# Sequences 1 to 3 of an SSD and MLP kernel: B by token through SBUF transfers, x by chunk, copies on other engines

## The chip, the cores and the metric

The kernel runs on one core of a Trainium2 chip. The metric is the time of one execution on the device in microseconds. Before the change it was 119.97 us, the median of 3 runs (119.9 to 120.58). The profile shows one execution that took 118.98 us, of which 117.0 us lie between its first and its last instruction (the span). The engines are named as in the profile: PE (matrix multiplication; PEld are its weight loads), DVE (vector engine), ACT (scalar engine), POOL, and SP, which here only issues transfers.

## What is computed

Two things in a row: a chunked state-space layer over 4 sequences with 8 heads, and a two-layer MLP on its result.

```
batch, H, S, D, N = 4, 8, 768, 32, 16
for each chunk:
    cum  = cumsum(log a)
    M    = (C B^T) * exp(cum_i - cum_j) * causal
    y    = M x + (C state) * exp(cum)
    state = exp(sum log a) * state + sum_j B_j x_j exp(cum_last - cum_j)
x2 = y as (3072 tokens, 256)
out = gelu_tanh(x2 @ w_in) @ w_out          # 256 -> 2048 -> 256
```

## The kernel before

The kernel takes chunks of 128 tokens, so that a sequence has 6 (`CPB`) and the whole input 24. Chunks are worked in units: unit 0 is chunk 0, unit 1 is chunk 1, and units 2 to 12 are two chunks each. Sequence b starts at chunk 6b; sequence 1 is units 4 to 6, and so on.

All work is first written down as nodes: a function, an engine, an assumed duration, the nodes it depends on. `run_order` then plays the nodes through in assumed time, with a priority for each node from the table `PRIO`, and the instructions are emitted in the order that comes out. Each engine runs its own list in that order. SP is one list too: loads and stores wait there one behind the other. Each transfer also waits until the transfer eight before it on the same list has landed, because eight completion counters are used in turn.

For a unit u the steps are:

- `f_G` (L659, PE): the products of C and B for each pair of heads, into the PSUM tile gb (four banks, one per head group).
- `f_M` (L669, DVE): gb times the causal mask, to the SBUF tile m.
- `f_D` (L680, PE): the chunk's contribution to the state, from B by token (the tile bn) and x, into a buffer of the ring hp.
- `f_S` and `f_SP` (L730, L737, DVE): the new state, and the state spread out over a block mask.
- `f_Y` (L702 and L711, PE): y from the state and from m and x, into the PSUM tile yb. From unit 4 on, Y of u, D of u + 1 and G of u + 1 are one block, `f_YDG`.
- `f_yev` (L720): yb copied to xm, the input of the MLP.
- `f_s1` (L757, PE): w_in times xm, into hp; `f_gelu` (L765, ACT): hp through gelu into gT. There are two hp buffers.
- `f_s2` (L774, PE): gT times w_out into o_ps (one bank) or yb; `f_oev` (L781, L783): that copied to SBUF; `f_store` (L787): to memory. The last chunk is done in two halves of 128 columns: `f_s2h`, `f_oevh`, `f_storeh` (L792 to L801).

For each sequence, B and C are scaled by the running products of a. For sequences 1 to 3 they come with tokens spread over partitions in a way that a 32 by 32 transpose on DVE can turn: `f_mulg` (L533) multiplies, `f_Tg` (L543) transposes to bh and ch (token along the free axis), `f_Fg` (L553) makes ce from ch. B by token, which `f_D` needs, is then made out of bh by PE: `f_N` (L625) is six transposes into gb, `f_bn` (L458 through `copy`, ACT) copies them to bn. Sequence 0 goes another way (`f_T`, `f_E`, `f_F`, and `f_N` for chunks 1 to 5).

x of sequences 1 to 3 comes as one transfer per sequence (`load_xs`, L353), x of sequence 0 unit by unit. `f_castx` (L460, POOL) casts it to bf16. `f_wi` and `f_wo` cast the weights, which come in quarters through six buffers wf; w_in quarters 2 and 3 are shared by POOL and DVE (L462).

While PE has nothing to do before the first s2, it is given fill multiplications (L1065).

Of the kernel before, what the change touches and what calls it, by code (L numbers as in the profile page):

```python
# [31 lines left out]
def run_order(nodes, pools, hop=0.08, same=0.04, idle=None, wait=()):  # L32
# [64 lines left out]
    'f_clip(0, 256)': 308.538, 'f_R(0,)': -15.941, 'f_clip(256, 384)': -339.826, 'f_RT0()': 1159.49,  # L97
    'f_R(1,)': 367.141, 'f_recip0()': -323.896, 'f_mul0(1,)': -323.906, 'f_mul0(0,)': -35.176,
    'f_T0(1,)': 1123.21, 'f_T0(0,)': 1159.5, 'f_ce0()': -138.371, 'f_bh0()': 266.725, 'f_R(2,)': 330.337,
    'f_G(0,)': -91.981, 'f_pe()': -193.992, 'f_RT()': 1125.27, 'f_M(0, 0, 0, 2)': -285.936,  # L100
    'f_M(0, 0, 2, 4)': 367.131, 'f_pp()': 1125.26, 'f_recip()': 468.131, "f_castx(0, 'ACT')": 266.715,
    'f_mul(1,)': -194.002, 'f_pend()': 270.364, 'f_Y(0,)': 1119.78, 'f_yev(0,)': 209.42,
    'f_mul(0,)': -35.176, 'f_T(1,)': 1152.81, "f_wi(0, 0, 2, 'POOL')": 97.158,
    "f_E(0, 1, 'ACT', 21, 64)": 270.354, 'f_T(0,)': 55.447, "f_E(0, 1, 'ACT', 64, 128)": 272.36,
    'f_F(0, 128, 384)': 468.121, 'f_D(0,)': 1170.19, 'f_s1(0, 0)': 1244.43,
    "f_E(0, 0, 'ACT', 21, 64)": -152.035, 'f_F(0, 384, 768)': -343.397, "f_wi(1, 0, 2, 'POOL')": 106.043,
    "f_E(0, 0, 'ACT', 64, 128)": 102.425, 'f_S(0, 0)': -318.328, 'f_G(1,)': 1209.63, 'f_SP(0,)': -323.654,
    'f_gelu(0, 0)': 267.9, 'f_N(0,)': 1123.2, "f_castx(1, 'POOL')": 106.053, 'f_M(1, 0, 0, 4)': -287.074,
    'f_s1(0, 1)': 1244.44, "f_bn(0, 'ACT')": 270.405, 'f_D(1,)': 1119.09, 'f_gelu(0, 1)': 103.579,
    'f_G(2,)': 379.65, "f_wi(2, 0, 1, 'POOL')": -96.227, "f_wi(2, 1, 2, 'DVE')": 244.836,  # L110
    'f_S(1, 0)': 509.234, 'f_Y(1,)': 1167.76, 'f_SP(1,)': -318.348, 'f_s1(0, 2)': -68.513,
    'f_yev(1,)': -185.791, "f_wi(3, 0, 1, 'POOL')": 97.168, "f_wi(3, 1, 2, 'DVE')": -166.728,
    'f_gelu(0, 2)': 88.559, 'f_M(2, 0, 0, 4)': 468.111, 'f_s1(0, 3)': 256.892, 'f_s1(1, 0)': -5.424,
    'f_gelu(0, 3)': 841.948, 'f_M(2, 1, 0, 4)': 286.612, "f_castx(2, 'POOL')": 106.083,
    'f_gelu(1, 0)': 209.42, 'f_s1(1, 1)': 1244.44, 'f_D(2,)': -72.563, 'f_gelu(1, 1)': 310.499,
    'f_G(3,)': 1170.77, "f_wo(0, 'POOL')": -6.862, 'f_S(2, 0)': -86.636, 'f_s1(1, 2)': 1167.75,
    'f_SP(2,)': -328.534, 'f_S(2, 1)': -166.718, 'f_Y(2,)': 1125.08, 'f_gelu(1, 2)': -187.491,
    'f_SP(3,)': -95.439, "f_wo(1, 'POOL')": 106.093, 'f_s1(1, 3)': 39.343, 'f_M(3, 0, 0, 4)': 471.605,
    'f_yev(2,)': 310.489, "f_s2(0, 0, 0, 'o')": 1244.43, "f_s2(0, 0, 1, 'o')": 1149.98,
    'f_gelu(1, 3)': 43.879, "f_wo(2, 'POOL')": 71.86, 'f_s1(2, 0)': 262.608, 'f_M(3, 1, 0, 4)': -59.147,  # L120
    'f_s1(2, 1)': 1158.13, 'f_gelu(2, 0)': 316.947, "f_s2(0, 0, 2, 'o')": -169.949,
    "f_wo(3, 'POOL')": -209.595, 'f_gelu(2, 1)': 45.731, 'f_s1(2, 2)': 1170.19, 'f_s1(2, 3)': -203.565,
    'f_gelu(2, 2)': -95.091, "f_s2(0, 0, 3, 'o')": 1161.73, "f_castx(3, 'POOL')": 106.073,
    'f_gelu(2, 3)': -187.501, 'f_s1(2, 4)': -116.936, 'f_clipg(1,)': -328.524, 'f_scang(1,)': -182.29,
    "f_oev(0, 'ACT')": 316.957, 'f_s1(2, 5)': -331.499, 'f_gelu(2, 4)': 69.73, 'f_rT(1,)': 1150.59,
    "f_s2(1, 0, 0, 'o')": -206.245, 'f_qT(1,)': -105.019, "f_s2(1, 0, 1, 'o')": 281.291,
    'f_gelu(2, 5)': -281.439, 'f_D(3,)': -165.791, 'f_s1(2, 6)': 215.528, 'f_mulg(1, 0, 0, 3)': -276.921,
    "f_s2(1, 0, 2, 'o')": 348.67, 'f_S(3, 0)': -197.187, 'f_gelu(2, 6)': -234.888,
    "f_s2(1, 0, 3, 'o')": -86.131, 'f_SP(4,)': -161.739, 'f_s1(2, 7)': -124.52,
    'f_mulg(1, 0, 3, 6)': -104.486, "f_oev(1, 'ACT')": 253.329, 'f_Y(3,)': -102.426, 'f_store(0,)': 1122.82,  # L130
    'f_gelu(2, 7)': -70.863, 'f_Tg(1, 0, 0, 3)': -94.76, "f_s2(2, 0, 0, 'o')": -163.857,
    'f_Tg(1, 0, 3, 6)': -94.74, 'f_yev(3,)': -250.819, "f_s2(2, 0, 1, 'o')": -198.132,
# [12 lines left out]
    'f_gelu(3, 5)': -106.495, 'f_SP(6,)': -136.64, "f_s2(3, 0, 1, 'o')": 253.321, 'f_s1(3, 6)': 85.42,
    'f_SP(7,)': -49.121, 'f_YDG(4,)': -223.29, 'f_scang(2,)': 68.177, 'f_gelu(3, 6)': -185.039,
    'f_rT(2,)': 65.364, 'f_s1(3, 7)': 213.456, 'f_S(5, 0)': -126.73, 'f_yev(4,)': 98.262,
    "f_s2(3, 0, 2, 'o')": 1165.93, 'f_store(3,)': -294.692, 'f_S(5, 1)': -120.802, 'f_gelu(3, 7)': -337.135,
    'f_mulg(2, 0, 3, 6)': -75.966, 'f_s1(4, 0)': 228.601, 'f_s1(4, 1)': 90.433, 'f_SP(9,)': -67.877,
    'f_gelu(4, 0)': -346.344, "f_s2(3, 0, 3, 'o')": 272.801, 'f_M(5, 0, 0, 4)': -66.78,  # L150
    'f_gelu(4, 1)': 58.961, 'f_s1(4, 2)': 1244.61, "f_oev(4, 'ACT')": 264.536, 'f_s1(4, 3)': -243.335,
    'f_gelu(4, 2)': 104.018, "f_s2(3, 1, 0, 'o')": 281.251, 'f_M(5, 1, 0, 4)': -146.018,
    "f_s2(3, 1, 1, 'o')": 282.52, 'f_gelu(4, 3)': 264.546, 'f_s1(4, 4)': 228.611, 'f_SP(8,)': -52.003,
    "f_castx(8, 'POOL')": -310.299, 'f_s1(4, 5)': -138.071, 'f_gelu(4, 4)': -233.107,
    "f_s2(3, 1, 2, 'o')": 316.331, 'f_mulg(2, 0, 0, 3)': -31.787, "f_castx(7, 'POOL')": 290.955,
    "f_s2(3, 1, 3, 'o')": 266.119, 'f_gelu(4, 5)': 344.271, 'f_Tg(2, 0, 3, 6)': 24.233,
    'f_s1(4, 6)': -159.257, "f_castx(9, 'POOL')": 297.549, 'f_Tg(2, 0, 0, 3)': 61.636,
    "f_oev(5, 'ACT')": 58.931, 'f_store(4,)': -314.436, 'f_YDG(5,)': 280.254, 'f_qT(2,)': 68.167,
    'f_gelu(4, 6)': 97.521, 'f_mulg(2, 1, 3, 6)': -119.373, 'f_s1(4, 7)': 282.53, 'f_S(6, 0)': -96.547,
    'f_yev(5,)': 9.537, "f_s2(4, 0, 0, 'o')": 1165.94, 'f_M(6, 0, 0, 4)': -96.449,  # L160
    "f_s2(4, 0, 1, 'o')": 1264.77, 'f_gelu(4, 7)': -346.334, 'f_s1(5, 0)': -163.07, 'f_s1(5, 1)': 269.011,
    'f_M(6, 1, 0, 4)': -258.554, 'f_gelu(5, 0)': -66.058, "f_s2(4, 0, 2, 'o')": 282.52,
    'f_store(5,)': -360.018, "f_s2(4, 0, 3, 'o')": 281.261, 'f_gelu(5, 1)': 206.319, 'f_s1(5, 2)': 292.499,
    'f_mulg(2, 1, 0, 3)': -53.518, "f_oev(6, 'ACT')": 206.339, 'f_s1(5, 3)': -242.892,
    'f_gelu(5, 2)': 417.866, 'f_Tg(2, 1, 0, 3)': 31.703, 'f_N(2,)': 287.685, 'f_SP(10,)': 40.492,
    "f_s2(4, 1, 0, 'o')": 294.667, 'f_gelu(5, 3)': -342.46, "f_s2(4, 1, 1, 'o')": -145.414,
    'f_Fg(2, 0, 3)': 40.502, "f_bn(2, 'ACT')": 52.208, 'f_s1(5, 4)': 266.109, 'f_Tg(2, 1, 3, 6)': 114.6,
    'f_s1(5, 5)': -159.026, 'f_Fg(2, 3, 6)': 1189.33, 'f_gelu(5, 4)': 195.675, "f_s2(4, 1, 2, 'o')": 389.998,
    'f_clipg(3,)': 1208.58, "f_s2(4, 1, 3, 'o')": -178.482, 'f_gelu(5, 5)': 398.02,
# [83 lines left out]
def kernel(  # L253
# [491 lines left out]
    def f_s1(u, i):  # L745
# [4 lines left out]
        if u not in gts:  # L750
            gts[u] = next_gt()
# [351 lines left out]
```

## Time and profile before

| what | value |
|---|---|
| median of 3 runs | 119.97 us |
| the profiled execution | 118.98 us |
| its span | 117.0 us |
| mean granted PE clock | 0.995 |
| s1, L757, 128x256 forms | x352, 47.8 us busy |
| s2, L774, into o_ps | x336, 44.4 us busy |
| gelu, L765 | x96, 53.6 us busy, 596 ns each |
| M, L669, 128x1024 | x23, 27.2 us busy, 1213 ns each |
| f_N of sequences 1 to 3, L625 into gb | x18 |
| f_bn of sequences 1 to 3, L458 from gb | x3, 815 ns each |
| transfers | 14.28 MB, mean 122 GB/s |

Busy times of PE overlap (a multiplication is counted from its start to the end of its pipeline), so 267 ns of mean length is not what one costs in a row: the chain shows eight 128x256 multiplications in 0.87 us.

The page cuts the span in 40 slices; a digit is the busy share of a slice in tenths:

```
PE   5899999999999999999999999999999999999980
DVE  3787999939699996994999693291919000000100
ACT  4123756765795778687666859667777776676610
POOL 7303735640032003200510000000000000000000
DMA  2998979968959497579611101101101101111111
```

Read from left to right, these rows show an opening of some seven slices, a middle in which PE is full and DVE nearly so, and an end in which only PE and ACT work. The DMA row falls away after slice 20, when all loads have come.

### The profile page before, as it was taken

The numbers are of one execution on the slowest core, as the hardware profiler recorded it, in microseconds if no ns is written. First come the engines' busy times: TensorE is split into PE (matmuls) and PEld (weight loads), VectorE is DVE, ScalarE is ACT, GpSimd is POOL, SyncE is SP. The second block draws the span as 40 slices with busy tenths as digits, with TensorE's granted clock in tenths as the row PEclk, the third lists the DMA queues.
The fourth block names the chain that finished last, engine by engine and source line by source line (L and its number), as shares of the span: only waits on it lengthen the run. The fifth ranks groups of instructions, "written<-read, shape, count | busy, mean of one in ns | idle before, by whom it ended". The sixth has DMA issues, their size and how long they took to land.

```text
span 117.0 us, 3536 instructions
## 1 busy us (share of the span) xinstructions
PE 111.7 (96%) x1484; PEld 98.9 (85%) x1484; DVE 71.2 (61%) x161; ACT 75.3 (64%) x145; POOL 18.1 (16%) x38
## 2 busy tenths in 40 slices
PE   5899999999999999999999999999999999999980
PEld 5788778997987897998989899898989899999970
DVE  3787999939699996994999693291919000000100
ACT  4123756795765778687666859667777776676610
POOL 7303735640032003200510000000000000000000
PEclk9999999999999999999999999999999999999998
DMA  2998979968959497579611101101101101111111
GB/s 49 251 287 233 364 180 375 313 153 188 207 137 218 112 210 169 117 186 208 172 46 45 44 7 45 41 12 45 50 0 45 50 0 44 45 50 45 46 47 45
DMA packets 44251, 14.28 MB, mean 122 GB/s; under 512 B 39052, under 2 KB 42700, under 8 KB 44236
## 3 DMA queue, kind: packets, MB, share of 16 engines
q1 hardware_dynamic: 43148, 13.95, 48.4%
q10 hardware_dynamic: 1088, 0.11, 0.7%
q8 instruction: 11, 0.18, 0.6%
q14 instruction: 4, 0.03, 0.1%
HBM read 10.91 MB, written 3.15 MB: 120 GB/s over the span
## 4 chain that ended last, share of the span: by engine, by line
PE 87%; DVE 7%; POOL 2%; issue 1%; ACT 1%; POOLq 0%; DVEq 0%; ACTq 0%
PE hp L757 35%; PE o_ps L774 31%; PE gb L659 3%; PE yb L774 3%; DVE m L669 3%; PE yb L711 3%; PE yb L702 3%; PE o_ps L1065 2%; PE gb L792 2%; DVE ce L619 1%; PE hp L492 1%; PE gb L625 1%; DVE sp_new L737 1%; DVE w_in_sb L462 1%; PE hp L680 1%
## 5 line engine op out<-in xcount | busy, mean ns | idle before, releaser
L765 ACT ACTIVATE gT<-hp 128x512 bf16<-128x512 f32 x96 | 53.6, 596 | 20.0 <-PE hp L757 19.9
L757 PE MATMUL hp<-xm,w_in_sb 128*128 128x256 bf16 (+1 forms) x416 | 53.0, 267 | 0.0
L757 PEld LDWEIGHTS <-w_in_sb 128*128 128x128 bf16 x416 | 42.0, 115 | 3.3 <-issue 2.1
L774 PE MATMUL o_ps<-w_out_sb,gT 128*128 128x256 bf16 x336 | 44.4, 273 | 0.0
L774 PEld LDWEIGHTS <-gT 128*128 128x128 bf16 x368 | 35.8, 98 | 3.6
L669 DVE TENSOR_TENSOR m<-gb,tri 128x1024 bf16<-128x1024 f32 (+1 forms) x25 | 28.5, 1171 | 0.0
L783 DVE COPY o_sb<-o_ps 128x256 f32<-128x256 f32 x1 | 0.4, 425 | 18.5 <-ACT gT L765 18.5
L781 ACT ACTIVATE o_sb<-o_ps 128x256 f32<-128x256 f32 x20 | 7.7, 386 | 4.9 <-ACT gT L765 3.2
L737 DVE SCALAR_TENSOR_TENSOR sp_new<-s_new,pend,bmask 128x256 bf16<-128x256 f32 x20 | 10.3, 526 | 0.3
L1065 PE MATMUL o_ps<-wz 128*128 128x128 bf16 x75 | 8.9, 281 | 1.3 <-DVE warm L364 1.3
L460 POOL CAST x<-xs_t 128x512 bf16<-128x512 f32 x9 | 5.6, 654 | 27.6 <-DMA xs_t<-in_x_dram 18.1
L730 DVE SCALAR_TENSOR_TENSOR s_new<-s_new,pend,hp 128x64 f32<-128x64 f32 x16 | 4.5, 279 | 7.3 <-PE hp L680 4.4
L720 ACT ACTIVATE xm<-yb 128x512 bf16<-128x512 f32 (+1 forms) x13 | 7.3, 563 | 2.4 <-PE yb L711 2.2
L1065 PEld LDWEIGHTS <-wz 128*128 128x128 bf16 x75 | 6.9, 129 | 1.6 <-DVE warm L364 1.3
L711 PE MATMUL yb<-m,x 128*32 128x128 bf16 x192 | 6.3, 223 | 0.0
L702 PE MATMUL yb<-ce,sp_new 128*32 128x128 bf16 x160 | 5.3, 221 | 0.0
L659 PE MATMUL gb<-ce,bh 32*128 32x256 bf16 x96 | 5.2, 282 | 0.1
L533 DVE TENSOR_TENSOR bc<-bc_t,rr 128x192 bf16<-128x192 f32 x12 | 4.6, 435 | 1.0 <-DMA bc_t<-in_C_dram 0.9
L460 POOL CAST w_in_sb<-wf 128x512 bf16<-128x512 f32 x6 | 3.7, 636 | 8.4 <-DMA wf<-in_moe_w_in_dram 8.4
L460 POOL CAST w_out_sb<-wf 128x1024 bf16<-128x1024 f32 x4 | 4.2, 1040 | 2.4 <-DMA wf<-in_moe_w_out_dram 2.4
L711 PEld LDWEIGHTS <-x 128*32 128x32 bf16 x192 | 3.8, 97 | 0.8 <-issue 0.8
L702 PEld LDWEIGHTS <-sp_new 128*32 128x32 bf16 x160 | 2.9, 96 | 1.7 <-issue 1.6
(83 smaller groups left out, 67.3 us busy)
## 6 DMA issues: line engine op xcount, KB each, us to landing
out_dram<-o_sb SPq DMA_DIRECT2D x23, 128.0 KB, 1.8
xs_t<-in_x_dram SPq DMA_DIRECT2D x3, 768.0 KB, 6.6
wf<-in_moe_w_in_dram SPq DMA_DIRECT2D x4, 512.0 KB, 7.0
wf<-in_moe_w_out_dram SPq DMA_DIRECT2D x4, 512.0 KB, 6.4
bc_t<-in_B_dram SPq DMA_DIRECT2D x12, 96.0 KB, 2.8
bc_t<-in_C_dram SPq DMA_DIRECT2D x12, 96.0 KB, 2.3
x_t<-in_x_dram SPq DMA_DIRECT2D x6, 128.0 KB, 7.3
bc_t<-in_C_dram SPq DMA_DIRECT2D x1, 384.0 KB
```

The lines of the kernel that those rows point to most:

```text
L460: nc.gpsimd.tensor_copy(out=o, in_=i)
L659: nc.tensor.matmul(out=gb[:, g, 256 * k:256 * k + 256], lhsT=bh_of(gc)[32 * g:32 * g + 32], rhs=ce_of(gc)[32 * g:32 * g + 32], start=True, ...
L669: nc.vector.tensor_tensor(out=MT[gc][:, g0:g1], in0=gb[:, g0:g1, 256 * k:256 * k + 256] .rearrange("p g (e t) -> p g e t", e=2), in1=tri_b ...
L702: nc.tensor.matmul(out=y4[32 * j:32 * j + 32, k, w], lhsT=sp[:, 32 * h:32 * h + 32], rhs=ce_of(gc)[:, h % 2], start=first(j), stop=False, ...
L711: nc.tensor.matmul(out=y4[32 * j:32 * j + 32, k, w], lhsT=X16[u][:, k, 32 * h:32 * h + 32], rhs=m[:, h // 2, h % 2, :], start=first(j), st ...
L720: nc.scalar.activation(xm[:, :, t0:t0 + n * Q].rearrange("p w (c t) -> p c w t", c=n), y4[:, 0:n], AF.Copy)
L737: nc.vector.scalar_tensor_tensor(out=sp_new.rearrange("p (g d) -> p g d", g=4), in0=state[("s", gc)].rearrange("p (o d) -> p o d", o=1).to ...
L757: nc.tensor.matmul(out=hp[:, j * nt:(j + 1) * nt], lhsT=w_in5[:, kc, fi // 4, fi % 4], rhs=xm[:, kc, t0:t0 + nt], start=(kc == 0), stop=(k ...
L765: nc.scalar.activation(gts[u][:, i * per:(i + 1) * per, 0:nt], hps.pop((u, i)).rearrange("p (j t) -> p j t", j=per), AF.Gelu_apprx_tanh)
L774: nc.tensor.matmul(out=ops[gc], lhsT=gts[u][:, fi, tt * Q:(tt + 1) * Q], rhs=w_out_sb[:, fi, :], start=(fi == 0), stop=(fi == NF - 1), ski ...
L781: nc.scalar.activation(o_sb, ops.pop(gc), AF.Copy)
L1065: nc.tensor.matmul(out=zb[:, 0:128], lhsT=wz[:, 0:128], rhs=wz[:, 0:128], start=True, stop=True)
```

## The change

- **B by token.** For sequences 1 to 3 `f_N` and `f_bn` go. After `f_mulg` of B, `f_bq` copies the scaled B into a tile bq in two strided halves (the first half of sequence 1's and both of the others' on POOL, one on ACT), and four transfers per sequence, `load_bn`, move it from SBUF to SBUF into bn, which now lies by head group. They are issued on SP. `f_D` reads bn there.
- **x by chunk.** x of sequences 1 to 3 is loaded in six transfers of 128 KB each instead of one. x of sequence 0 lies in one tile of six chunks. The order of the loads comes from the priorities: the first chunks of x come before B of sequence 0, and two more x chunks come before the last quarter of w_in and of w_out.
- **Buffers.** wf is one tile of six slots with fixed places, which also holds x, B and C of sequence 3 later; gT is three tiles that hold two units each; bn has a buffer for each sequence.
- **Output of chunks 0 and 1.** They share the one bank of o_ps, each in its half, and their s2 are interleaved.
- **Last halves.** `f_s2h` writes into the two buffers of hp instead of gb.
- **Copies' engines.** Each copy may now run on several engines; the table `ENG` picks one. To DVE go eight output copies, three x casts, three half quarters of w_out, two of the four `f_E` copies of sequence 0, and the last `f_yev`; to ACT go the output copy of chunk 21, two x casts and halves of w_in quarters 0 and 3. All priorities are new.

```diff
-    next_bn = ring(const, 2, [128, CPB, 128], BF16, "bn")
+    next_bn = ring(const, batch, [128, CPB * 128], BF16, "bn")
+    next_bq = ring(const, 2, [128, R, CPB, 2 * N], BF16, "bq")
...
-    def load_xs(b):
-        XF[("s", b)] = ldxs.tile([128, H * CPB, D], FP32, name="xs_t")
-        nc.sync.dma_start(out=XF[("s", b)], in_=bass.AP(
-            tensor=x.tensor, offset=x.offset + b * H * S * D, ap=[[D, Q], [Q * D, H * CPB], [1, D]]))
+    def load_xs(b, c):
+        XF[("s", b)] = xst[b - 1].rearrange("p (k d) -> p k d", d=D)
+        nc.sync.dma_start(out=XF[("s", b)].rearrange("p (h c) d -> p c h d", c=CPB)[:, c],
+                          in_=x[b, :, c * Q:(c + 1) * Q, :].rearrange("h p d -> p h d"))
...
+    def f_bq(b, k, eng):
+
+
+        if k == 0:
+            U[b]["bq"] = next_bq()
+        copy(eng, U[b]["bq"].rearrange("p (s k) c n -> p k s c n", k=2)[:, k],
+             bc16_of(b, 0).rearrange("p (c s n k) -> p k s c n", s=2, n=2 * N, k=2)[:, k])
+
+    def load_bn(b, g):
+
+        d = U[b]
+        if "bn" not in d:
+            d["bn"] = next_bn()
+        nc.sync.dma_start(out=d["bn"][:, 192 * g:192 * g + 192],
+                          in_=d["bq"][32 * g:32 * g + 32].rearrange("p r c n -> p r (c n)"))
...
     def f_s2h(h):
+        ops[("h", h)] = next_hp()[:, 0:128]
         for f in range(NF):
-            nc.tensor.matmul(out=gb[:, 2 * h, 0:128], lhsT=gts[NU - 1][:, f, Q:2 * Q],
+            nc.tensor.matmul(out=ops[("h", h)], lhsT=gts[len(BLOCKS) - 1][:, f, Q:2 * Q],
                              rhs=w_out_sb[:, f, 128 * h:128 * h + 128], start=(f == 0),
-                             stop=(f == NF - 1), skip_group_check=True)
+                             stop=(f == NF - 1))
...
-        nn = add("PE", 0.34, f_N, b, deps=ts, prio=q + 15.6)
-        bb = add("ACT", 0.75, f_bn, b, "ACT", deps=[nn], prio=-45)
-        nn.takes("gram", bb)
-        for c in range(CPB):
-            bnn[CPB * b + c] = bb
+        bq = []
+        for k in range(2):
+            bq.append(any_of({"ACT": 0.6, "POOL": 0.8, "DVE": 0.5}, f_bq, b, k, deps=mb + bq, prio=q - 0.5))
+        for n in bnl[b]:
+            n.deps += bq
...
+ENG = {
+    'f_castx(1,)': 'ACT', 'f_E(0, 1, 64, 128)': 'DVE', 'f_wi(0, 1)': 'ACT', 'f_E(0, 0, 21, 64)': 'DVE',
+    'f_wi(3, 1)': 'ACT', 'f_wo(0, 1)': 'DVE', 'f_wo(2, 0)': 'DVE', 'f_wo(3, 0)': 'DVE', 'f_oev(1,)': 'DVE',
+    'f_bq(1, 0)': 'POOL', 'f_castx(5,)': 'ACT', 'f_castx(7,)': 'DVE', 'f_bq(2, 0)': 'POOL',
+    'f_oev(5,)': 'DVE', 'f_bq(2, 1)': 'POOL', 'f_castx(8,)': 'DVE', 'f_castx(9,)': 'DVE',
+    'f_bq(3, 0)': 'POOL', 'f_oev(9,)': 'DVE', 'f_bq(3, 1)': 'POOL', 'f_oev(11,)': 'DVE', 'f_oev(12,)': 'DVE',
+    'f_oev(16,)': 'DVE', 'f_oev(17,)': 'DVE', 'f_yev(12,)': 'DVE', 'f_oev(20,)': 'DVE', 'f_oev(21,)': 'ACT',
+}
```

## The prediction

> **What bounds the kernel now.** The page first: shares of engines, and shares of the chain that ended last.
>
> ```profile
> PE 111.7 (96%) x1484; PEld 98.9 (85%) x1484; DVE 71.2 (61%) x161; ACT 75.3 (64%) x145; POOL 18.1 (16%) x38
> ...
> PE 87%; DVE 7%; POOL 2%; issue 1%; ACT 1%; POOLq 0%; DVEq 0%; ACTq 0%
> ```
>
> TensorE holds the chain, but not all the time, so I read the chain in order of time (start, length, engine, tile, line):
>
> ```profile
> 11.69 1.65 DVE ce L619 x4
> ...
> 15.14 0.24 issue
> 15.38 0.29 DVE s_new L730
> 15.69 0.48 DVE sp_new L737
> 16.17 0.75 DVE w_in_sb L462
> 16.93 2.27 DVE m L669 x2
> ...
> 30.41 0.34 PE gb L625 x6
> ...
> 36.02 0.17 PE hp L680 x8
> ...
> 50.13 0.34 PE gb L625 x6
> ...
> 71.00 0.33 PE gb L625 x6
> ...
> 111.77 1.80 PE gb L792 x32
> 113.66 0.30 DVE o_sb L462
> 114.03 0.28 ACT o_sb L458
> ```
>
> Three stages are to be seen. Until about 19.2 us DVE leads (after loads) and PE's fill multiplications only pass the time. From 19.24 to 113.57 us every piece is PE's, back to back, so here a microsecond of PE work removed is one gained, and any wait of PE is lost for good. Then a tail: two copies one behind the other, and a store, to the span's end at 117.0.
>
> Third, the busy time of the engines in stretches, because the change gives DVE more work (columns: PE, PEld, DVE, ACT, POOL busy, clock, DMA):
>
> ```profile
> 25.00:30.00 5.00, 5.00 (x74) 4.08 (x73) 4.00 (x12) 3.60 (x8) 0.61 (x1) 1.00 0.92 189
> 30.00:35.00 5.00, 5.00 (x55) 4.36 (x54) 4.15 (x11) 3.34 (x7) 1.05 (x2) 1.00 0.89 169
> 35.00:45.00 10.00, 10.00 (x130) 8.72 (x127) 9.79 (x24) 6.98 (x14) 0.74 (x2) 1.00 0.93 187
> 60.00:70.00 10.00, 10.00 (x159) 8.81 (x146) 9.00 (x20) 7.35 (x14) 0.00 (x0) 1.00 0.09 28
> ```
>
> DVE has 0.2 us to spare in 35 to 45 and 1.0 in 60 to 70, and PE still never waits.
>
> **The change part by part.**
>
> *Transposes out (f_N, f_bn).* Eighteen L625 transposes leave PE: 0.34 + 0.34 + 0.33 = 1.01 us of the gapless chain. Three bn copies (0.81 us each) leave ACT, which is busy 64%, so they count nothing. All other PE counts are the same in both orders (416 of s1, 368 + 32 of s2, 192 + 160 of Y, 96 of G, 80 of D), but for 8 fills fewer before 20 us. Gain 1.01.
>
> *Last halves in two buffers.* Now both halves lie in one tile, gb. The DVE copy starts 0.09 us after the last of 32 L792 multiplications although its own half was done 0.9 us earlier, and the ACT copy starts only when DVE's has ended. With a tile for each half, DVE copies beneath the second half and ACT starts where DVE did: 114.03 - 113.66 = 0.37 us gained. The store behind it is the same.
>
> *B by token.* In place of a PE pass, two strided copies (bq) per sequence and four SBUF-to-SBUF transfers on SP's queue. No row shows a 128x384 bf16 copy on POOL; POOL's 128x512 cast at 0.65 bounds it above, ACT's 128x384 copy of 0.49 below. The tightest use is sequence 1's: its B multiplication ends on DVE at 29.2, PE needs bn at 36.02. In the new DVE order a w_out cast (which waits for its load) and an output copy stand ahead of that multiplication's second half: 0.4 + 0.4, so 30.0. POOL's bq 0.65, ACT's 0.4 behind it: 31.1. On SP the first transfer waits for bq, and with it everything queued behind: two stores between the four transfers, then two x chunks and the next sequence's a, B and C. Six issues at 0.41 to 0.50 (stores 0.41, bc loads 2.0 for 4) make 33.7. Landing: nearest rows are stores (1.8) and 96 KB loads of B (2.8), so 35.5 to 36.5 against 36.0. I take 0, the middle of the margin: the four multiplications of a chunk each need one transfer only, the last of them the last. Bounds: nothing, to 0.5, and 2 more if SP is held as at 27.86, where two stores took 5.19. It can't be below nothing, since PE needs bn no earlier than before. Sequences 2 and 3 have 10 us between multiplication and use; covered.
>
> The Trainium skill bears on this path, in "DMA: Bandwidth & Descriptors", section "Specifications": transfers under 512 bytes a piece miss the line rate; these pieces are 384 bytes. Its section on small descriptors says that SBUF-to-SBUF transfers don't pay that. By the first rule I would put all of them at the 2.8 end, a stall of 0.5; by the second at the 1.8 end, none.
>
> *x by chunk.* Three 768 KB loads become 18 of 128 KB: the same bytes, 15 more issues at 0.47 (7 us of SP's time); with the 12 of bn SP issues 27 more. SP stands idle or waiting for output from 55 us on, and before that its loads run ahead of use by several us. In the opening x chunks 0 and 1 now precede B, so w_in quarters 0 and 1 come one chunk later (0.6 us at the 216 GB/s that the DMA rows show while x moves), and quarter 3 three chunks, 1.8. Before, POOL had quarter 3 at 15.99; 17.8 now, and its second half is cast by ACT, which waits for the load with two gelus behind it, on which PE's s1 depends: 17.8 + 0.6 = 18.4. The s1 that needs it stands just ahead of the Y of unit 2, which waits for DVE until 20.3, and unit 0's fourth s1 was moved behind that Y. Covered; I count nothing, bounds 0 and 0.6 (quarter 0 late at PE's first s1). Later, ACT's cast of unit 5's x waits for the chunk issued last, behind bn: 34.6 + 0.6 + 2.8 = 38.0 at most, about 0.7 after its turn, with gelus behind it; ACT's gaps of 0.28 to 0.66 there take up most of it.
>
> *Opening on DVE.* Gone: two w_in casts, 0.24 + 0.75 on the chain. Added ahead of M(1): two copies out of PSUM of 128x384 and 128x258 bf16. DVE's 128x256 copy out of PSUM took 0.43, ACT's forms 0.49 and 0.39; so 0.55 + 0.43 = 0.98. They cancel; bounds -0.4 (copies hide in the 0.81 us that DVE waits at 11.7) and +0.4 (the second one waits for ACT, which now has a w_in cast of 0.6 between).
>
> *Copies moved.* Net seven output copies and one yev more on DVE, three x casts and three w_out casts. In 20 to 70: four output copies of 0.43 and six casts. A cast's price depends on its neighbour:
>
> ```profile
> 15.05 0.42 DVE L462 CAST w_in_sb<-wf 128x512 bf16<-128x512 f32 x1
> 16.09 0.83 DVE L462 CAST w_in_sb<-wf 128x512 bf16<-128x512 f32 x1
> 57.73 1.45 DVE L533 TENSOR_TENSOR bc<-bc_t,rr 128x192 bf16<-128x192 f32 x2
> ```
>
> The second cast ran while POOL cast (15.99 to 16.64), the pair in the third line, elsewhere 0.64, within POOL's three casts from 56.91 to 58.96. So DVE gains 1.7 + 2.5 to 5.0 = 4.2 to 6.7 us where it idled 7.2 of 50 (the stretches of 20 to 70 us sum to 42.8). I count nothing, since M's are spaced by PE's own progress and the sum still fits.
>
> "SBUF — State Buffer" of the Trainium skill, section "Who interferes with whom", makes this a lock: the later of the two engines blocks fully. By it the second cast would have ended at 16.64 + 0.42 = 17.06; the next instruction on the chain starts at 16.93, so the trace nearly agrees. Its lock would put each added cast that starts under one of POOL's at up to 0.65 + 0.42 = 1.07.
>
> **Sum.** The profiled execution took 118.98, of which 117.0 is span; 118.98 - 1.01 - 0.37 = 117.6. The median of the runs is 119.97, 0.99 above that execution; the same difference on it gives 118.59.
>
> **The rivals.**
>
> 1. *A late arrival takes back the gain* (bn, w_out quarter 3, which now queues behind five more loads and which DVE waits for ahead of B's multiplication, or unit 5's x). For: the margin of -0.5 to +0.5 above, and DMA at 0.9 until 45 us. Against: PE's work before the use grows by nothing, and only sequence 1 is tight. Price 0.5 to 1.4: 119.1 to 120.0, within 1%.
>
> 2. *DVE becomes the bound: slower.* Place: Y(u) waits for M and sp in 25 to 70 us. Where the added work exceeds DVE's idle time of the stretch it is late: 25 to 35, an output copy and a cast, 0.85 to 1.26 against 1.85, none; 35 to 45, the same against 0.2, about 0.85; 60 to 70, two output copies, 0.86 against 1.0, none. To that come POOL's five bq copies: in 56.91 to 58.96 POOL's 2.05 us cost DVE 0.81 on the pair and 0.3 on the next sp, so five at 0.65 cost 1.7; and half of the other five casts' stretch (5 x 0.41), 1.0. Together 3.55, less 1.38: 122.1; it turns slower than before from 1.4 us of waiting on, by over 1% from 2.6. For: a single engine, in order, at 98%. Against: the casts and output copies were not all put in the full stretches, and copies in SBUF give way by tenths, while ACT, which feeds the same PE, gets lighter.
>
> 3. *The halves still run one behind the other* (a wait at tile level stays): the 0.37 is not had, 118.96.
>
> **How the numbers follow.** A run of this kernel can tell about 1% from no change: 118.77 to 121.17 is "same". Forecast 0.52, own range 118.1 to 119.0 (the opening's bounds), four fifths of it below 118.77; rival 1 0.22; rival 2 0.19, nearly all over 121.17; rival 3 0.07. Faster: 0.52 x 0.8 = 0.42, and 0.02 for an opening that gains more: 0.44. Slower 0.18. Same 0.38. The range reaches over the forecast, rivals 1 and 3: 118.0 to 120.4.
>
> **What would show it.** Right: no L625-like transposes after 20 us; PE gapless from about 20.3 to 112.5; the last ACT copy 0.1 us behind the last PE piece while DVE's lies before it; PE's busy time about 1 us less. Rival 1: PE weight loads of the D line waiting for a bn transfer near 36 us, or s2 for a w_out cast near 28. Rival 2: Y's PE lines waiting for DVE, DVE at 10 of 10 in 25 to 70. The prediction is wrong if PE's first Y of unit 2 starts more than 0.5 us from 20.3, or if waits of PE after it exceed 0.5 us in sum.

## The result: slower by 3%, and the profile after

The changed kernel took 124.02 us, the median of 4 runs (122.96 to 124.62), against 120.28 us for the kernel before (119.9 to 120.74). The ratio is 1.030, with a 95% interval of 1.022 to 1.038. The forecast of 118.6 us was wrong, and so was the range up to 120.4. Here and below a ratio is taken over the executions within 1.5% of the shortest of their kernel, which leaves out two of four for token_alone, seven of ten for casts_pool, four of twelve for all_casts_pool, three of twelve for token_a_halves and one of four for load_order, mended and a_late.

The profiled execution has a span of 122.2 us, 5.2 more than before. The page's shares of engines and of the chain:

```profile
PE 111.3 (91%) x1458; PEld 97.6 (80%) x1458; DVE 75.0 (61%) x175; ACT 72.1 (59%) x137; POOL 17.7 (14%) x39
...
PE 60%; SPq 15%; DMA 14%; DVE 3%; ACT 2%; POOL 2%; issue 1%; ACTq 0%; POOLq 0%
```

PE held 87% of the chain before; now it holds 60%, and 29% lie with SP's list of transfers and with transfers in flight. What PE waited for between 19 and 60 us (line that waited, who released it, us in total, times, longest):

```profile
PE o_ps L821 <- DVE o_sb L486: 1.5, 1, 1.5
PE hp L801 <- POOL w_in_sb L484: 1.0, 1, 1.0
PE hp L801 <- DVE s_new L774: 0.8, 1, 0.8
PE o_ps L821 <- DVE w_out_sb L486: 0.7, 1, 0.7
PE hp L725 <- ACT x L482: 0.7, 1, 0.7
PE hp L725 <- DMA bn<-bq: 0.2, 1, 0.2
```

The same view of the kernel before is empty. Only the last line names a transfer, but the chain, in order of time, shows that transfers stand behind the others:

```profile
16.50 6.18 DMA wf<-in_moe_w_out_dram
...
24.90 5.06 DMA bct<-in_B_dram
...
39.42 3.48 DMA at<-in_a_dram
...
48.89 2.94 DMA xs<-in_x_dram
51.83 0.37 DVE bh L569
52.20 0.32 DVE o_sb L486
52.56 1.03 PE o_ps L821 x8
...
117.15 1.80 PE hp L837 x32
...
119.03 0.28 ACT o_sb L482
```

DVE's own instructions, one by one, show how a load reaches PE through a copy that has nothing to do with it (start, length, operation, and in brackets the idle time before and its releaser):

```profile
42.92 0.23 DVE L526 TENSOR_SCALAR at<-at 128x128 f32<-128x128 f32 x1 [2.17 <-DMA at<-in_a_dram]
...
49.92 0.43 DVE L486 CAST x<-xs 128x512 bf16<-128x512 f32 x1 [2.78 <-DMA xs<-in_x_dram]
```

At 40.75 DVE has come to the first step of sequence 2, which needs a. It stands there for 2.17 us, and the two s_new of unit 5 behind it are late: PE waits 0.83 us. At 47.1 it has come to the cast of unit 7's x, which POOL did before. It stands 2.78 us, and the output copy, seven instructions further on, is late: PE waits 1.48 us, for the one bank of o_ps.

Why the loads are late, SP's entries show (start, time until the last of them is issued):

```profile
7.46 6.99 SPq L359 DMA_DIRECT2D xe<-in_x_dram  x3
14.49 1.45 SPq L475 DMA_DIRECT2D wf<-in_moe_w_in_dram  x1
```

The last quarter of w_in is issued at 14.49 us behind three x chunks that took SP 6.99 us, the second of them 1.95 and the third 4.48. The wait for the transfer eight back did not hold them: the two transfers in question had landed by 5.91 and 6.50, and SP's waits up to 57 us name no transfer. Three loads of 512 KB stand just ahead of the three chunks; more on this at the end. Before, all four quarters had been issued by 8.2. POOL casts the quarter at 20.21 instead of 15.99, and PE waits 1.04 us for it. The a of sequence 2 is issued at 39.42 instead of 33.10.

DVE is not the bound. The stretches that answer those of before (PE, PEld, DVE, ACT, POOL busy, clock, DMA):

```profile
35.00:45.00 10.00, 8.28 (x114) 6.50 (x113) 6.67 (x17) 5.25 (x11) 0.90 (x1) 1.00 0.58 135
60.00:70.00 10.00, 10.00 (x130) 8.95 (x123) 8.90 (x21) 6.41 (x12) 2.89 (x5) 1.00 0.75 147
```

Where DVE had 9.79 of 10 us before, it has 6.67 now, and the DMA engines are busy for 0.58 instead of 0.93 of the time. Full is only SP's list: in its waits up to 57 us I count 3.9 us for other engines, none over 1.0, where it was 13.8 before, in pieces of up to 4.4, nearly all of it for copies of output. By 57 us SP has issued 66 entries instead of 56. These and the entries that took long used up the slack; but the slack had stood at stores, and not ahead of the loads that come due first.

The sum of the 5.2 us: Y of unit 2 begins at 21.45 instead of 20.25 (+1.2); PE's waits after that are 3.9 instead of 0; PE's pieces between, from that Y to PE's end without the waits, take 93.6 instead of 93.3 (+0.3); and PE's end to the end of the span is 3.2 instead of 3.4 (-0.2).

### The profile page after: what moved, and what is told of

Read it like the earlier page. It is cut to its first block, busy times and chain, and to the rows that moved or that the text cites. A ratio compares the mean times of both kernels' runs of the same rounds, so it can differ in the third digit from the quotient of the medians.

```text
span 122.2 us, 3528 instructions
## 1 busy us (share of the span) xinstructions
PE 111.3 (91%) x1458; PEld 97.6 (80%) x1458; DVE 75.0 (61%) x175; ACT 72.1 (59%) x137; POOL 17.7 (14%) x39
## 2 busy tenths in 40 slices
DMA packets 46219, 14.87 MB, mean 122 GB/s; under 512 B 41020, under 2 KB 44668, under 8 KB 46204
## 4 chain that ended last, share of the span: by engine, by line
PE 60%; SPq 15%; DMA 14%; DVE 3%; ACT 2%; POOL 2%; issue 1%; ACTq 0%; POOLq 0%
PE hp L801 26%; PE o_ps L821 24%; SPq L359 7%; DMA wf<-in_moe_w_out_dram 5%; DMA bct<-in_B_dram 4%; PE yb L821 3%; DMA at<-in_a_dram 3%; SPq L475 2%; DMA xs<-in_x_dram 2%; SPq L385 2%; PE gb L704 2%; POOL w_out_sb L484 2%; PE yb L747 2%; PE hp L837 1%; PE yb L756 1%; SPq L355 1%
## 5 line engine op out<-in xcount | busy, mean ns | idle before, releaser
L821 PE MATMUL o_ps<-w_out_sb,gT 128*128 128x256 bf16 x336 | 45.4, 273 | 2.3 <-DVE o_sb L486 1.5
L781 DVE SCALAR_TENSOR_TENSOR sp_new<-s_new,pend,bmask 128x256 bf16<-128x256 f32 x20 | 9.6, 487 | 0.2
L1153 PE MATMUL o_ps<-wz 128*128 128x128 bf16 x67 | 8.2, 293 | 1.3 <-DVE warm L396 1.3
L482 ACT ACTIVATE o_sb<-o_ps 128x256 f32<-128x256 f32 x14 | 5.4, 385 | 5.2 <-DVE o_sb L486 1.8
L482 ACT ACTIVATE xm<-yb 128x512 bf16<-128x512 f32 (+1 forms) x12 | 6.7, 560 | 2.2 <-PE hp L725 1.2
L486 DVE COPY o_sb<-o_ps 128x256 f32<-128x256 f32 x7 | 2.9, 420 | 4.3 <-PE o_ps L821 4.3
L484 POOL CAST w_out_sb<-wf 128x512 bf16<-128x512 f32 x5 | 3.7, 756 | 4.6 <-DMA wf<-in_moe_w_out_dram 4.5
L484 POOL COPY bq<-bc 128x384 bf16<-128x384 bf16 x5 | 2.5, 528 | 12.2 <-DVE bc L559 12.2
```

The lines of the kernel that those rows point to most:

```text
L482: nc.scalar.activation(o, i, AF.Copy)
L484: nc.gpsimd.tensor_copy(out=o, in_=i)
L781: nc.vector.scalar_tensor_tensor(out=sp_new.rearrange("p (g d) -> p g d", g=4), in0=state[("s", gc)].rearrange("p (o d) -> p o d", o=1).to ...
L821: nc.tensor.matmul(out=ops[gc], lhsT=gts[v][:, fi, tt * Q:(tt + 1) * Q], rhs=w_out_sb[:, fi, :], start=(fi == 0 and gc != 1), stop=(fi == ...
L1153: nc.tensor.matmul(out=zb[:, 0:128], lhsT=wz[:, 0:128], rhs=wz[:, 0:128], start=True, stop=True)
```

## The experiments

Three theories were set against one another. **SP's list**: 27 more entries of about 0.5 us make each later load late. **Order**: single loads were put behind others. **Engines**: casts that wait for loads moved from POOL, where a wait held nobody up, to DVE and ACT, whose lists hold other work. The Trainium skill, "Perfetto Trace Analysis", section "What 'DMA-bound' means", has a rule near the first: a kernel can be bound on the issuing engine, whose track is then solid, and large descriptors are what matters there. SP's track is nearly solid here (3.9 us of waits for engines in 57). The first experiment makes x's transfers large, but not their pieces (45979 DMA packets on the page instead of 46219), so it tests the number of entries and not that rule.

In each kernel the order of all instructions is written out as a list, as the planner gave it, so that an edit moves only what it names. The diffs of such lists are shortened: they show the places that change, engine by engine, and a line can stand for several entries. The results together; columns 2 to 5 are from the profile, in us: the start of Y of unit 2, PE's waits after that in sum, PE's end, the span. The last is the ratio to the kernel before, with its interval.

| kernel | Y of unit 2 | waits | PE's end | span | ratio |
|---|---|---|---|---|---|
| before | 20.25 | 0 | 113.6 | 117.0 | |
| changed | 21.45 | 3.9 | 118.9 | 122.2 | 1.030 (1.022 to 1.038) |
| x_whole | 22.28 | 4.4 | 122.4 | 125.2 | 1.057 (1.050 to 1.065) |
| load_order | 22.47 | 2.1 | 118.4 | 121.6 | 1.025 (1.018 to 1.033) |
| casts_pool | 21.60 | 1.8 | 116.5 | 119.4 | 1.013 (1.006 to 1.021) |
| mended | 23.26 | 1.2 | 117.4 | 120.3 | 1.023 (1.016 to 1.029) |
| opening_alone | 23.08 | 2.7 | 119.0 | 122.2 | 1.028 (1.024 to 1.032) |
| mended_opening | 23.05 | 1.0 | 117.0 | 119.9 | 1.009 (1.006 to 1.012) |
| all_casts_pool | 20.73 | 2.5 | 116.0 | 118.9 | 1.000 (0.996 to 1.003) |
| token_alone | 21.08 | 2.3 | 117.7 | 122.0 | 1.022 (1.009 to 1.034) |
| a_late | 20.92 | 3.2 | 117.7 | 121.1 | 1.025 (1.018 to 1.033) |
| token_a_first | 20.45 | 1.4 | 114.9 | 118.5 | 1.004 (1.001 to 1.007) |
| token_a_halves | 20.77 | 1.4 | 115.1 | 118.0 | 0.995 (0.992 to 0.999) |
| token_moved | 20.50 | 1.2 | 114.6 | 117.6 | 0.996 (0.994 to 0.999) |

The profile is of one execution each, and Y of unit 2 varies by itself: it came at 20.25 to 21.08 in the kernel before and the five made from it, which share its opening, and at 21.45 to 23.26 in the four that share the changed kernel's order of loads there (changed, x_whole, casts_pool, mended).

**Whole loads of x (x_whole).**

```diff
     def load_xs(b, c):
         XF[("s", b)] = xst[b - 1].rearrange("p (k d) -> p k d", d=D)
-        nc.sync.dma_start(out=XF[("s", b)].rearrange("p (h c) d -> p c h d", c=CPB)[:, c],
-                          in_=x[b, :, c * Q:(c + 1) * Q, :].rearrange("h p d -> p h d"))
+        if c == 0:
+            nc.sync.dma_start(out=XF[("s", b)], in_=bass.AP(
+                tensor=x.tensor, offset=x.offset + b * H * S * D, ap=[[D, Q], [Q * D, H * CPB], [1, D]]))
```

> The changed kernel with its order of instructions written out, but x of each of sequences 1 to 3 comes in one transfer of 768 KB again, at the place of its first chunk and behind C: 15 issues on SP less. What is computed is the same. Span of the changed kernel 122.2 us, PE's waits after 19 us 4.95 us: 1.04 for w_in, 0.71 for w_out, 0.21 for bn, 0.68 for unit 5's x, 0.83 for s_new (behind DVE's wait for a of sequence 2), 1.48 for an output copy (behind DVE's wait for unit 7's x). Theory 'SP's list': SP issues one entry after the other without idling from the start to 66 us and each later load is late because it stands behind 27 more entries of 0.5 us; with 15 fewer, the last three waits (0.68 + 0.83 + 1.48) go, the first two stay: span 119.2. Theory 'order': the loads are late because single ones were put behind others, and only the x of unit 5 changes here: 121.5. Theory 'engines': DVE and ACT wait in their lists for loads that POOL waited for before; the wait for x on DVE stays or grows, as it now needs the whole sequence: 121.5 to 122.5.

It became slower still: 127.29 us. The waits for unit 5's x and for w_out are gone, those for w_in and bn grew (1.63 and 0.44), and DVE stood 4.8 us for the whole of sequence 2's x and PE 3.45 us behind it, with 3.41 us at half clock after that: a cast on DVE wants two chunks and gets them with the last of six. This is what "engines" said. It also shows that the number of entries is not what makes the load of a late. Five entries fewer stand ahead of a of sequence 2 on SP, and it was issued at 39.19, where the changed kernel had 39.42, because SP came to the first bn sooner and stood there for bq (its longest wait up to 60 us, and its entry for a):

```profile
SPq L673 <- ACT bq L483: 4.6, 1, 4.6
...
39.19 0.59 SPq L369 DMA_DIRECT2D at<-in_a_dram  x1
```

**Three loads earlier (load_order).**

```diff
 SP:
+load_wi(3)
 load_x(4), load_x(2), load_x(3)
-load_wi(3)
 load_wo(0), load_wo(1), load_wo(2)
+load_wo(3)
...
-load_wo(3)
...
+load_xs(1, 2)
 load_xs(1, 3), load_xs(1, 4)
...
-load_xs(1, 2)
```

> The changed kernel with its order written out and three loads moved on SP: w_in quarter 3 ahead of x chunk 4, w_out quarter 3 right behind quarter 2, chunk 2 of sequence 1's x ahead of chunk 3. The number of transfers is the same and all work is done. Theory 'order': the waits for w_in (1.04), w_out (0.71) and unit 5's x (0.68) go, and the later two go with them because DVE is not set back: span 117.2 to 118. Theory 'SP's list': those three go, but a of sequence 2 and x of sequence 2 are no earlier, 0.83 + 1.48 stay: 119.8. Theory 'engines': the same 119.8, since what DVE waits for at 50 us is not moved.

After the opening it came as "SP's list" and "engines" said: the waits for w_out and unit 5's x are gone, 0.81 for a and 1.12 for the output copy stay. But in the opening the wait only changed hands: unit 2's x now lands behind w_in, POOL stands 3.64 us for it, and PE waits 2.15 us instead of 1.04. With 3.41 us at half clock behind that, the span is 121.6 and not 119.8.

**Casts back on POOL (casts_pool).**

```diff
 ENG = {
-    'f_wi(3, 1)': 'ACT', 'f_wo(0, 1)': 'DVE', 'f_wo(2, 0)': 'DVE', 'f_wo(3, 0)': 'DVE',
-    'f_castx(5,)': 'ACT', 'f_castx(7,)': 'DVE', 'f_castx(8,)': 'DVE', 'f_castx(9,)': 'DVE',
```

> The changed kernel with its order written out, and eight casts that wait for loads put back on POOL: x of units 5, 7, 8 and 9, both halves of w_out that DVE had in quarters 2 and 3 and one of quarter 0, and the half of w_in quarter 3 that ACT had. All else, SP's list too, is the same and all work is done. Theory 'engines': the loads are as late as before but nothing queues behind them any more: the waits of 0.71, 0.68 and 1.48 go, span 119.3. Theory 'SP's list' and theory 'order': PE needs the data itself; the waits for w_in and w_out stay or grow by one more cast of 0.65 on POOL, only the 1.48 goes because DVE is free of x of unit 7: 120.7 to 121.5.

The profiled execution has the span that "engines" gave, 119.4 for 119.3, but in part by luck. With SP's list untouched the waits of 0.71 and 1.48 are gone, as "engines" said. Those for data that PE needs itself grew, as the other two said: unit 5's x from 0.68 to 1.01, w_in from 1.04 to 1.20. PE's waits after 19 us fell by 1.9 us and the span by 2.8; the rest is in PE's pieces (93.1 instead of 93.6) and in the tail. The ten times run from 121.1 to 123.8, eight of them from 122.9 up, and the profile is of one of 121.12. The median of all ten is 2.3% over the kernel before, so the gain on the longer ones is smaller, and their waits were not seen.

**B by token alone, in the kernel before (token_alone).**

```diff
-f_N(b), f_bn(b)
+f_bq(b, 0), f_bq(b, 1)
 SP:
 load_xs(1)
+load_bn(1, 0..3)
 f_store(0), f_store(1), load_a(2), load_bcg(2, 0, 0..3)
```

> The kernel before with its order written out, and only B by token through transfers: f_N and f_bn of sequences 1 to 3 left out of it, two bq copies each (POOL, one of sequence 1's on ACT) and four transfers on SP, for sequence 1 ahead of the first store, for the others behind a store. One bq buffer, the zero tile of the fill multiplications cut to the 128 columns that are read. All work is done. Span of before 117.0. The step of the prediction (transposes out, bn in time): 116.0. Theory 'SP's list': before, SP stood waiting for output copies (5.2 and 3.9 us), so 12 entries more are hidden: 116.0 to 116.4. If the transfers of bn are themselves what is late: PE waits at D of sequence 1 near 36 us, 117.0 or more.

Neither: bn was in time, yet the kernel lost 2.2% (its four times run from 121.88 to 125.16, and the ratio is that of two, 121.88 and 123.62; the profile is that of 123.98, so what follows is not shown for the shortest). SP waits for bq until 30.65 and needs 4.6 us for the four transfers; a of sequence 2, behind them, is issued at 36.49 instead of 33.10. DVE stands 2.62 us for it, PE 1.78 at 40.65. This became the theory for the rest: **what is late is whatever is queued on SP behind the waiting transfer, and what pays is the engine that stands in order for it.**

**Only a later, nothing of the change (a_late).**

```diff
 SP:
 f_store(0), f_store(1)
+load_bcg(2, 0, 0..3), load_bcg(2, 1, 0), load_bcg(2, 1, 1)
 load_a(2)
-load_bcg(2, 0, 0..3), load_bcg(2, 1, 0), load_bcg(2, 1, 1)
```

> The kernel before with its order written out and nothing of the change; on SP, six of the eight loads of B and C of sequence 2 go ahead of a of sequence 2, which so is issued some 3 us later. All work is done. Theory 'DVE stands for a': with no transfer of bn at all, DVE waits 2 to 3 us for a near 36 us, PE 1.0 to 1.8 us behind it near 40 us; if PE's wait is 1.8 or more, 3.41 us of half clock follow, 1.7 us more: the time is 1.0 to 3.5 us over before. If the later a is hidden by DVE's other work: no wait of PE, the time of before.

The kernel before, with one load of 64 KB some 3 us further back on SP (issued at 37.37 instead of 33.10), is slower by 2.5%. The waits of PE from 19 to 60 us:

```profile
PE hp L757 <- DVE s_new L730: 2.7, 1, 2.7
PE o_ps L774 <- POOL w_out_sb L460: 0.5, 1, 0.5
```

It is the wait of token_alone without any transfer of bn. The load had no lead to spare. (The slow clock did not follow here; see the end.)

**a first (token_a_first).**

```diff
 SP:
+load_a(2)
 load_xs(1)
 load_bn(1, 0..3)
 f_store(0), f_store(1)
-load_a(2)
```

> The kernel before with B by token alone, and one load moved on SP: a of sequence 2 ahead of x of sequence 1, so ahead of the transfers of bn, which wait for bq. All work is done. With B by token alone and a behind bn, DVE stood 2.62 us for a, PE 1.78 us behind it, and 3.41 us at half clock followed. Theory 'SP's list stands behind bq': that wait and the slow clock go, no other takes their place: PE's waits after 19 us under 1.0 in sum, span 2.5 to 3.5 under that run's 122.0, so 118.5 to 119.5, and below before by 1.0 if the opening goes alike. Theory 'bn itself': D of sequence 1 waits for bn near 37 us, the span stays at 121 or more.

The wait for a is gone, the span is 118.5, in the range. Against token_alone the one moved load is worth about 1.8% (1.004 after 1.022, whose interval is wide). Below before it did not come: waits of 0.91 for w_out and 0.46 for bn of sequence 2 took the place, 1.4 in sum where under 1.0 was expected.

**a first, and the last halves in two buffers (token_a_halves).**

```diff
 def f_s2h(h):
+    ops[("h", h)] = next_hp()[:, 0:128]
...
-            nc.tensor.matmul(out=gb[:, 2 * h, 0:128], lhsT=gts[NU - 1][:, f, Q:2 * Q],
+            nc.tensor.matmul(out=ops[("h", h)], lhsT=gts[NU - 1][:, f, Q:2 * Q],
```

> The same kernel as the one with a of sequence 2 first, and the last halves in the two buffers of hp instead of gb. All work is done. By the prediction's step the last copy begins 0.37 us nearer to PE's end: PE's end to ACT's copy 0.08 instead of 0.46, the median 0.3 to 0.4 under that of the kernel without it and 1.0 to 1.4 under before. Rival of the prediction (halves serial at tile level): no difference. If the store sets the end and not the copies: ACT's copy is earlier and the end is not.

This version comes out half a per cent under the kernel before: 119.85 us against 120.33, ratio 0.995 (0.992 to 0.999). ACT's copy begins 0.07 us behind PE's last piece (115.18 after 115.11), as in the changed kernel, where without the buffers it was 0.45 behind. The median fell by 0.7 us, more than the 0.37 of the copies; PE's end to the span's end went from 3.65 to 2.9, so the store's landing has a part in it that one profile each can't settle.

**Two moves more (token_moved).** bq(1, 1) on POOL, bn of sequence 2 three entries earlier.

> The kernel before with B by token, a of sequence 2 first and the last halves in two buffers, and two things moved: sequence 1's second bq copy from ACT to POOL (the output copy behind it on ACT kept PE waiting 0.76 us at 31.6), and sequence 2's transfers of bn three entries earlier on SP, ahead of a store (PE waited 0.46 us for them at 55.5 in the run without the halves). All work is done. If these waits are bn's own: both go, median 0.4 to 0.9 us under the kernel without the moves, ratio to before 0.988 to 0.992. If SP or POOL only hand the lateness on (bn of sequence 1 later by POOL's second copy of 0.5): a wait at D of sequence 1 near 37 us, the ratio stays at 0.995.

Both waits went, and 0.35 for ce and 0.69 for bn of sequence 1 came: 0.996, no further gain. The lateness was handed on.

**Casts on POOL and three loads earlier (mended).** The edit of casts_pool, with load_wo(3) behind load_wo(2), load_xs(1, 2) ahead of load_xs(1, 3) and load_a(2) ahead of both.

> The changed kernel with its order written out, the eight casts back on POOL, and three loads earlier on SP: w_out quarter 3 right behind quarter 2, chunk 2 of sequence 1's x ahead of chunk 3, a of sequence 2 ahead of both. All work is done. Theory 'late loads block DVE and ACT' (order and engines together): of the waits after 22 us, those for w_out, for unit 5's x and for a go, and the output copy's at 52 too: only bn's 0.2 is left, PE's waits after 22 us 0.5 or less, span 118.0 to 119.0. Theory 'SP's list is full': something else on SP is late in turn (bn or B of sequence 2), and 1 to 2 us of waits come back at 38 to 55 us: 119.5 to 121.

After 22 us the waits fell from 3.9 to 1.2, most of what is left for unit 5's x (0.77). But the opening was worse: PE waited 0.99 and 1.38 for w_in, and Y of unit 2 came at 23.26. The edit did not do that: up to w_out quarter 3 at 17.8 us SP's list is that of casts_pool, and the casts are on the same engines, yet w_in quarter 0 landed at 12.05 instead of 10.61. Why it landed later is open.

**The opening's loads as before (mended_opening, opening_alone).** The first is mended, the second the changed kernel, each with:

```diff
 SP:
-bc(0,1) x0 x1 bc(0,0) wi0 wi1 wi2 x4 x2 x3 wi3 wo0 wo1 wo2 x5
+bc(0,1) bc(0,0) x0 wi0 wi1 x1 wi2 wi3 x2 x3 wo0 wo1 wo2 x4 x5
 POOL:
-castx(2), wi(3, 0)
+wi(3, 0), castx(2)
```

> The mended kernel with the loads of the opening in the order that they have in the kernel before: B of sequence 0 ahead of x, x chunk 1 behind w_in quarter 1, w_in quarter 3 ahead of x chunks 2 and 3, all of w_out ahead of x chunks 4 and 5; on POOL the two casts of w_in quarter 3 ahead of unit 2's x. All work is done. Mended, the waits after 22 us were 1.2 in sum, but Y of unit 2 began at 23.26 instead of 20.25, with half clock from 14.5 to 21.5 behind waits of 0.99 and 1.38 for w_in. Theory 'order of the opening's loads': Y of unit 2 at 20.3 to 21.1 as in the kernels made from before, span 117 to 118, median 119.0 to 120.3. Rival 'opening's copies and fills' (two E copies on DVE, 8 fills fewer, w_in on ACT): Y of unit 2 stays at 21.5 or later and the span over 118.5.

> The changed kernel with only the opening's loads in the order of the kernel before (and the two casts of w_in quarter 3 ahead of unit 2's x). All work is done. Theory 'two separate losses': Y of unit 2 at 20.3 to 21.1 instead of 21.45, the wait of 1.04 for w_in gone; what comes later stays, waits of 3 to 4 us between 22 and 55: span 121 to 121.5. If the later waits hang on the opening (everything on SP a little earlier): 118 to 120. Rival 'opening's copies and fills': Y of unit 2 unchanged, 122.2.

Both missed on Y of unit 2: 23.05 and 23.08. Again a load stood in front of an engine: x chunk 1 now comes behind w_in quarter 1, and the changed kernel casts it on ACT. From ACT's instructions of mended_opening:

```profile
12.90 0.42 ACT L475 ACTIVATE x<-xe 128x256 bf16<-128x256 f32 x1 [4.64 <-DMA xe<-in_x_dram]
```

PE's transposes waited 1.95 us for the copy behind it. After the opening the two differ as they should: 1.0 us of waits with the later loads mended, 2.7 without. So most of the later waits don't hang on the opening; against the changed kernel's 3.9, the 0.71 for w_out went with it, and the output copy's fell from 1.48 to 0.91.

**The last two such casts on POOL too (all_casts_pool).**

```diff
 ENG = {
-    'f_castx(1,)': 'ACT', 'f_wi(0, 1)': 'ACT',
```

In POOL's list unit 1's x comes behind the casts of w_in quarters 0 and 1.

> The mended kernel with the opening's loads in the order of before, and the last two casts that waited for loads on ACT, unit 1's x and half of w_in quarter 0, put on POOL. All work is done. With these loads moved, ACT stood 4.64 us for x chunk 1 until 12.9 and PE 1.95 us behind ACT's copies; Y of unit 2 began at 23.05. Theory 'an in-order engine stands for a load': that wait goes, Y of unit 2 at 20.3 to 21.3 as in the kernels made from before, and with the rest as mended the span is 117 to 118, median 119.0 to 120.0, ratio to before 0.985 to 1.0. Rival 'opening's copies and fills' (two E copies on DVE, 8 fills fewer): Y of unit 2 stays at 21.5 or later, ratio 1.0 to 1.01.

Y of unit 2 is at 20.73, as in the kernels made from before, and the ratio is 1.000 (0.996 to 1.003); the median of all twelve times, 120.79 against 120.62, says the same, though four of them lie at 121.5 to 123.5. The whole 3% is accounted for by where loads stand on SP and on which engine the casts behind them stand, the two together; B by token, x by chunk, the output copies on DVE, the E copies on DVE and the two buffers are all still in. The rival (the opening's copies and fills) falls. What keeps it from being faster, PE's waits again:

```profile
PE hp L718 <- POOL x L477: 2.3, 2, 1.5
PE hp L718 <- DMA bn<-bq: 0.2, 1, 0.2
```

Unit 3's x, whose two chunks now stand behind all of w_out on SP, is late by 1.53 us, unit 5's by 0.77.

## Why the prediction was wrong, step by step

- **The step that failed** is the sentence under "x by chunk": "before that its loads run ahead of use by several us". It let 27 more entries on SP count nothing. The loads had next to no lead: a_late issued one load 4.3 us later than before and lost 2.69 us of PE's time. The changed kernel is 6.3 us late with that load. In x_whole, without 15 of the entries, it is 6.1 us late: what holds it is the transfer of bn that waits for bq, which the sum had seen and priced for bn alone. Both signs that the prediction named for being wrong came, Y of unit 2 at 21.45 and 3.9 us of waits after it.
- **w_in quarter 3, "Covered; I count nothing".** PE waited 1.04 for it, and Y of unit 2 came 1.2 later. I had put three x chunks at the mean rate of DMA, 1.8 us; they held SP for 6.99 us, though the transfers eight back had landed. The cast came 4.2 us later than before, not 1.8.
- **Rival 1, the late arrival,** was the right mechanism at 0.22, and its three places were right: bn 0.21, w_out 0.71, unit 5's x 0.68 ("ACT's gaps take up most of it" was wrong, ACT stood 1.99 us). Together that is 1.6 for the 0.5 to 1.4 priced. The others, a of sequence 2 (0.83) and unit 7's x (1.48), I had named as queued behind or as a cast moved, and priced neither as a wait of DVE. In "Copies moved" each cast was costed by its busy time; that DVE stands in order for the load was left out. It stood 2.78 us at unit 7's x and 1.71 at a w_out cast. Casts_pool shows that the waits of 1.48 and 0.71 come from there; how the 3% divides between the casts' engines and the order of loads is not shown, since no kernel has all ten casts on POOL and the changed order.
- **Bn itself** came out within its bounds, 0.21 us at D of sequence 1 against 0 to 0.5, and a transfer landed in 2.0 us; but the 0.21 is luck. bq was done at 33.7 instead of 31.1 and the last transfer landed at 38.9 instead of 35.5 to 36.5; PE itself came to D 2.7 us late, at 38.74 instead of 36.02.
- **Transposes out, -1.01.** They are gone, but the gain is not seen alone. PE's time from Y of unit 2 to its end without waits is 93.3 before, 93.6 in the changed kernel, 92.9 to 93.0 in the three token kernels without a slow clock, 92.7 in all_casts_pool. So 0.3 to 0.6 was seen, and pieces beside a wait stretch (eight s2 took 1.13 us at 30.11 instead of 0.87).
- **Last halves, -0.37.** Right: ACT's copy lies 0.08 us behind PE instead of 0.46, rival 3 falls. But it hangs at the end of whatever came before.
- **Rival 2, DVE as the bound** (0.19, the only case on the slow side by more than 1%), has the sign and is not what happened: DVE is emptier than before, 6.67 of 10 us where it had 9.79.
- **The base.** The profiled execution of before, with no wait of PE after 19 us, is the shortest seen of that kernel: others had spans of 117.3 to 119.5. I carried the difference of 0.99 to the median as a constant. It is part of the same matter: small waits for w_out of 0.5 to 0.9 stand in all the profiles of kernels made from it except token_moved's, where it is 0.20.

What stays open: the longer times of casts_pool and all_casts_pool, what makes single entries on SP take up to 4.5 us, the 0.35 us of the tail beyond the copies, and whether an order exists in which the changed kernel has neither of the waits left in all_casts_pool.

## What to carry to other kernels

A queue that issues in order is a resource with its own lead: for every entry added, ask which load behind it has the least lead, and read that lead from the trace (landing against first use), not from the DMA engines' share. An instruction that waits for a load costs its engine the wait, not its busy time, so put it on the engine whose list can stand still. A profile without a single wait may be the luckiest execution of a kernel that is close to several.

## What the hardware showed that I had not expected

**A short wait can cost twice.** In token_alone, after PE's wait of 1.78 us at 40.65 (columns as above; the clock is the number ahead of the last two):

```profile
41.00:42.00 1.00, 1.00 (x43) 0.57 (x40) 0.97 (x3) 0.72 (x2) 0.00 (x0) 1.00 0.87 242
42.00:43.00 1.00, 1.00 (x10) 0.75 (x7) 0.96 (x5) 0.37 (x2) 0.00 (x0) 0.59 0.78 177
43.00:44.00 1.00, 1.00 (x6) 0.73 (x5) 1.00 (x3) 0.59 (x1) 0.00 (x0) 0.50 0.18 29
```

The granted clock fell to 0.5 for 3.41 us, about 1.7 us of work lost. The same length followed waits of 2.15 (load_order) and 3.45 us (x_whole), but not those of 2.69 (a_late) and 1.48 (the changed kernel). The clock of a trace changes in steps of 3.41 us, and if these steps are continued back over the wait, the part of it that lies in one step sorts the cases: 1.78 us (token_alone), 2.15 (load_order) and 2.28 (x_whole) were followed by half clock, while a_late's wait is cut into 1.17 and 1.52 and the changed kernel's is 1.48. From these cases the line lies between 1.5 and 1.8 us of one step; in the opening it does not hold (mended lost the clock after 1.39). In the opening the full clock came to stay at 12.0 to 14.9 us in most kernels, but only at 19.2 to 21.5 in opening_alone, mended_opening and mended, where PE had waited 1.0 to 2.1 us at a time between 11 and 16; eight s1 of 128 columns took 1.04 us there instead of 0.61. The Trainium skill, "TensorE: Matmul & The Clock Gate", section "What's actually happening", says that a window of 3413 ns runs free of the kernel and that an idle window of about that length halves the clock. The length agrees, and a free-running window fits the way the waits fall into steps; that a whole idle window is needed does not agree, as 1.78 us were enough.

**Behind a large load the next issue is slow.** In token_alone the first bn, next on SP behind the 768 KB load of x, took 2.70 us to issue, with bq done at 30.65 and the transfer eight back landed at 26.83; the three behind it took 0.60 each. In the changed kernel, behind chunks of 128 KB, the first bn took 0.64. The x chunks of 1.95 and 4.48 us in its opening, behind three loads of 512 KB, look like the same thing. What SP waits for there the traces don't show, and x by chunk was not tested by itself.
